# Moving the contiguous DRAM copies of streamed weights from the first step to steps 2 to 6

## The chip, the cores and the metric

The kernel runs on one core of a Trainium2 chip. The metric is the device time of one execution in microseconds; lower is better. Three runs of the kernel before took 3726.68, 3730.98 and 3731.62 us, median 3730.98.

## The reference, cut to what matters

Four layers run over a sequence of 2048 positions with 640 channels, alternating between a memory-augmented recurrent attention (A) and a local dilated attention (B):

```
x = x + A(layernorm(x)); x = x + B(layernorm(x))
x = x + A(layernorm(x)); x = x + B(layernorm(x))

A:  for each of 64 segments of 32 positions:
      h = concat(mem (8 rows), xs (32 rows))              # 40 x 640
      q, k, v = h @ Wq, h @ Wk, h @ Wv                    # 32 heads of 192
      o = softmax(mask(q k^T * 192**-0.5)) v ;  o = o @ Wo
      mem = o[:8] ; out = o[8:]
B:  32 heads of 20, each position looks at 8 positions, 2 apart
```

Both A layers use the same weights. The memory of a segment is made by the segment before it, so the segments come one after the other.

## The kernel before

One step of the outer loop in `run` takes one segment of the first A layer and, two steps behind it (`LAG = 2`), one segment of the second, side by side as two lanes of one tile (`ST`). There are 66 such steps with A work, numbered from 0 in the code, so the first step is step 0; one more step finishes layer B.

A's weights are 16 units each of Wq, Wk, Wv and Wo, cut into 64 "halves" of 128 x 1920 elements in bf16, 480 KB each. 31 of them (`RESIDENT`) stay in SBUF from step 0 on, in tiles `res`. The other 33 are streamed again in every step through `ring`, a pool of five buffers (`RING = 5`) with tiles named `wt`. `resident_halves` chooses the streamed ones so that they lie evenly along the step's work: it walks the list `PLAN` in the order in which PE uses the halves and drops one whenever enough columns of work have gone by.

A half in its original place in DRAM is strided: `load_direct` reads it as rows of 384 elements from Wq, Wk and Wv, five to a partition, or of 640 elements from Wo, three to a partition. In step 0 the kernel loads all 64 halves that way. Each streamed half is then written once from its ring buffer to a contiguous DRAM tile `Wr[h]`, by a DMA that GpSimd (POOL) issues (L238). From step 1 on, the streamed halves are read from `Wr[h]` (L240), one run of 3840 bytes per partition. All loads are issued by SyncE (SP), in one queue (L225, L240, and L251 for the input x).

A ring buffer may be loaded again only when PE has read its half and, where there is a copy out of it, when that copy has landed. The order of PE's work is written out by hand in `PLAN` (`manual_schedule` for PE); the order on the other engines comes from the scheduler of the tile framework. POOL has other work too, in the same in-order queue as its DMA issues: the squares for the layer norms (`sq`, L283, used by `ln1` and `ln2`), one lane of `prod` (L445) and copies into `ST`, `kh` and `vh`. Other lines that are spoken of below: L313 (q and k), L361 (v), L395 (the output projection, `acc`), L405 and L402 (the cast of the new memory from `acc` into `ST`, which ends a step), L485 (DVE reductions of layer B).

Of the kernel before, what the change touches and what calls it, by code (L numbers as in the profile page):

```python
# [41 lines left out]
BPAD = (BW - 1) * BDIL  # L42
SCB = float(BDH) ** -0.5
LAG = 2

N_HALVES = 64
N_RESIDENT = 31
# [24 lines left out]
def resident_halves():  # L72

    order, t = [], 0
    for what, i in PLAN:
        for h in ([2 * i, 2 * i + 1] if what == "q" else [{"v": 32, "o": 48}[what] + i] if what in "vo" else [None]):
            t += COLUMNS.get(what, 0)
            if h is not None:
                order.append((h, t))
    kept, n = set(), 0  # L80
    for h, at in order:
        if (N_HALVES - N_RESIDENT) * at >= (n + 0.5) * t:
            n += 1
        else:
            kept.add(h)
    assert len(kept) == N_RESIDENT
    return kept


RESIDENT = resident_halves()  # L90


def window(ap, l):
# [23 lines left out]
class Kernel:  # L117
# [109 lines left out]
    def half(self, h):  # L227
        if h in self.resident:
            return self.resident[h]
        if h in RESIDENT:  # L230
            t = self.res.tile([P, HALF], BF16, name=f"res{h}")
            self.load_direct(t, h)
            self.resident[h] = t
            return t
        t = self.ring.tile([P, HALF], BF16, name="wt")
        if self.step == 0:
            self.load_direct(t, h)
            self.nc.gpsimd.dma_start(out=self.Wr[h][:, :], in_=t[:, :])  # L238
        else:
            self.nc.sync.dma_start(out=t[:, :], in_=self.Wr[h][:, :])  # L240
        return t
# [156 lines left out]
    def finish_step(self):  # L398
        nc, s = self.nc, self.step
        nxt = self.ST[(s + 1) % 2]  # L400
        if s + 1 == LAG:
            nc.vector.tensor_copy(out=nxt[:, :, 0, 0:NM], in_=self.acc[:, :, 0, 0:NM])  # L402
# [7 lines left out]
        else:  # L410
            ra = self.zero[:, :, :]
        rb = self.x2[:, :, :] if s >= LAG else self.zero[:, :, :]
        for l, r in ((0, ra), (1, rb)):
# [34 lines left out]
    def b_logits(self):  # L448
# [8 lines left out]
        src = ps[:, :, :]  # L457
        for l, at in ((0, 1), (1, 1 + LAG)):
            if self.step == at:
# [27 lines left out]
    def b_wo(self):  # L487
# [6 lines left out]
        if s <= self.n_seg:  # L494
            x2 = self.w2.tile([P, NCH, SEG], BF16, name="x2")
            nc.vector.tensor_tensor(out=x2[:, :, :], in0=ps[:, :, 0, :], in1=self.xr[:, :, 0, :], op=ALU.add)  # L496
            self.x2_next = x2
        k = s - 1 - LAG
        if k >= 0:
# [12 lines left out]
    def store(self):  # L512
        nc = self.nc
        k = self.step - 1 - LAG
        if k < 0 or k % 4 != 3:
# [9 lines left out]
    def run(self):  # L525
        nc, tc = self.nc, self.tc
        self.resident, self.xt, self.vts, self.ots = {}, {}, {}, {}
        self.Wr = {h: self.dram.tile([P, HALF], BF16, name=f"Wr{h}") for h in range(N_HALVES) if h not in RESIDENT}
        self.kh = self.vh = None
        self.x2 = self.x2_next = None  # L530
        self.step = 0
        with tc.manual_schedule(engines={PE}):
# [3 lines left out]
            self.alpha_x(0)  # L536
            n_steps = self.n_seg + LAG
            attend = {"q": self.qk, "s": self.scores, "t": self.p_transpose, "v": self.v, "pv": self.pv, "o": self.o}
# [80 lines left out]
```

## Time and profile before

| what | value |
|---|---|
| median of three runs | 3730.98 us |
| span of the profiled execution | 3732.1 us |
| PE busy | 3430.9 us, 92% |
| DVE busy | 2077.9 us, 56% |
| DMA, SyncE's queue | 1091.82 MB, 86.2% of 16 engines' span |
| DMA, POOL's queue | 16.22 MB, 1.1% |
| mean DMA rate | 301 GB/s |
| mean granted TensorE clock | 0.984 |

The profiled execution is given by its span from the first to the last instruction; no other time of that execution is shown, and the span lies 0.5 us above the slowest of the three runs. A busy share is the share of the span in which an engine has at least one instruction under way. The DMA share is the mean busy share of the core's 16 DMA engines; it can read a little over 1. The granted clock is the share of TensorE's full clock. A time "to landing" runs from the issue of a DMA to the completion of its transfer. In a list of groups "x33" counts instructions, and in a list of waits the three numbers are the total wait in us, how many, and the longest.

### The profile page before, as it was taken

Reading aid. Unit: us, or ns where it says so; the run is one execution under the profiler, and the core shown is the slowest. Engines: PE = TensorE matmul, PEld = TensorE weight load, DVE = VectorE, ACT = ScalarE, POOL = GpSimd, SP = SyncE. Lnnn points to the kernel's source line nnn. Section 1 sums busy time; section 2 is a strip of 40 time slices with the busy share of each in tenths; the row PEclk is TensorE's granted clock in tenths of the full one; section 3 lists DMA queues with packets and bytes.
Section 4 is the critical chain, followed back from the end, with each engine's and each line's share of the span. In section 5 each row is a group of like instructions: output and inputs, shape, how many; then the busy total and the mean of one; then the engine's idle time right before and its main releaser. Section 6 shows DMA issues by size and latency. Waiting matters only on the chain.

```text
span 3732.1 us, 170184 instructions
## 1 busy us (share of the span) xinstructions
PE 3430.9 (92%) x78045; PEld 2929.7 (79%) x78045; DVE 2077.9 (56%) x4858; ACT 1493.5 (40%) x3213; POOL 365.5 (10%) x467
## 2 busy tenths in 40 slices
PE   5799999999999999999999999999999999999997
PEld 3588788788788878778887887887888788788886
DVE  1355555655555555655556565555555555555555
ACT  1243444444444344444434444444443444444443
POOL 2110010011011001011100100100110010011000
PEclk7899999999999999999999999999999999999998
DMA  9988888888888889889888888888888888888885
GB/s 351 343 297 296 295 302 304 297 305 293 304 301 302 304 296 306 297 299 307 300 307 301 303 301 291 307 291 303 305 301 302 303 307 297 306 296 300 304 304 193
DMA packets 356064, 1121.56 MB, mean 301 GB/s; under 512 B 36424, under 2 KB 78032, under 8 KB 355344
## 3 DMA queue, kind: packets, MB, share of 16 engines
q1 hardware_dynamic: 350400, 1091.82, 86.2%
q0 software_dynamic: 2640, 16.22, 1.1%
q8 instruction: 610, 9.99, 1.1%
q10 hardware_dynamic: 2304, 2.62, 0.2%
q14 instruction: 110, 0.90, 0.1%
HBM read 1091.68 MB, written 18.84 MB: 298 GB/s over the span
## 4 chain that ended last, share of the span: by engine, by line
PE 66%; DVE 21%; DMA 7%; ACT 2%; issue 2%; SPq 1%; POOLq 0%; DVEq 0%; POOL 0%; ACTq 0%
PE qk_ps L313 23%; PE v_ps L361 18%; PE acc L395 11%; DVE oT L485 5%; DVE prod L483 4%; PE qkv_ps L438 4%; PE s_ps L331 3%; PE s_ps L325 2%; DVE vt L367 2%; PE o_ps L378 2%; DMA x_sb<-in_A_x_dram 2%; DMA wt<-Wr 2%; PE y_ps L492 1%; DVE sb L335 1%; DVE mx L337 1%
## 5 line engine op out<-in xcount | busy, mean ns | idle before, releaser
L315 ACT CAST QK<-qk_ps 128x480 bf16<-128x480 f32 x1056 | 586.9, 556 | 1197.9 <-PE qk_ps L313 1190.2
L313 PE MATMUL qk_ps<-ST,res 128*128 128x80 bf16 x17820 | 800.2, 203 | 56.1 <-DVE ST L405 21.3
L361 PE MATMUL v_ps<-wt,ST 128*128 128x384 bf16 x3630 | 706.2, 328 | 134.8 <-DVE vt L367 124.3
L313 PEld LDWEIGHTS <-res 128*128 128x128 bf16 x17820 | 724.8, 100 | 97.9 <-issue 49.4
L361 PEld LDWEIGHTS <-ST 128*128 128x128 bf16 x5280 | 475.0, 99 | 410.5 <-issue 150.3
L313 PE MATMUL qk_ps<-ST,wt 128*128 128x80 bf16 x13860 | 646.8, 203 | 15.8 <-DMA wt<-in_A_Wq_dram 8.0
L313 PEld LDWEIGHTS <-wt 128*128 128x128 bf16 x13860 | 575.9, 100 | 68.7 <-DMA wt<-in_A_Wq_dram 9.0
L367 DVE CAST vt<-v_ps 128x384 bf16<-128x384 f32 x528 | 289.8, 549 | 542.8 <-PE v_ps L361 541.4
L395 PE MATMUL acc<-ot,wt 128*128 128x80 bf16 x7920 | 375.8, 203 | 17.8 <-DMA wt<-in_A_Wo_dram 6.7
L395 PE MATMUL acc<-ot,res 128*128 128x80 bf16 x7920 | 364.3, 203 | 11.2 <-issue 6.0
L395 PEld LDWEIGHTS <-res 128*128 128x128 bf16 x7920 | 328.4, 100 | 42.0 <-DMA res<-in_A_Wo_dram 7.1
L365 ACT CAST vt<-v_ps 128x384 bf16<-128x384 f32 x528 | 250.1, 474 | 266.4 <-PE v_ps L361 262.2
L395 PEld LDWEIGHTS <-wt 128*128 128x128 bf16 x7920 | 317.7, 100 | 30.8 <-issue 8.6
L381 ACT CAST ot<-o_ps 128x480 bf16<-128x480 f32 x528 | 275.0, 560 | 162.2 <-PE o_ps L378 162.1
L485 DVE TENSOR_REDUCE oT<-prod 128x64 bf16<-128x512 bf16 x330 | 335.1, 1016 | 2.2
L361 PE MATMUL v_ps<-res,ST 128*128 128x384 bf16 x1650 | 328.4, 330 | 6.2 <-DMA res<-in_A_Wv_dram 4.2
L445 POOL TENSOR_TENSOR prod<-qT,kh 128x1280 bf16<-128x1280 bf16 x66 | 204.4, 3097 | 684.1 <-ACT kh L440 684.1
L335 DVE TENSOR_TENSOR sb<-s_ps,maskA 128x320 f32<-128x320 f32 x264 | 129.3, 490 | 212.3 <-PE s_ps L331 212.3
L283 POOL TENSOR_TENSOR sq<-x 128x160 f32<-128x160 bf16 x64 | 28.9, 452 | 2095.3 <-DVE x L496 2095.3
L483 DVE TENSOR_TENSOR prod<-bc_ps,vh 128x512 bf16<-128x512 f32 x330 | 222.8, 675 | 9.9 <-PE bc_ps L480 1.6
L353 ACT COPY PT<-pt_ps 64x320 bf16<-64x320 bf16 x264 | 110.9, 420 | 242.0 <-DVE PT L352 239.1
L341 DVE TENSOR_REDUCE sm<-sb 128x8 f32<-128x320 f32 x264 | 127.7, 484 | 107.2 <-ACT sb L339 107.2
(113 smaller groups left out, 3320.1 us busy)
## 6 DMA issues: line engine op xcount, KB each, us to landing
wt<-Wr SPq DMA_DIRECT2D x2145, 480.0 KB, 5.2
Wr<-wt POOLq DMA_DIRECT2D x33, 480.0 KB, 6.7
wt<-in_A_Wv_dram SPq DMA_DIRECT2D x11, 480.0 KB, 10.3
res<-in_A_Wk_dram SPq DMA_DIRECT2D x9, 480.0 KB, 10.7
res<-in_A_Wq_dram SPq DMA_DIRECT2D x9, 480.0 KB, 10.4
wt<-in_A_Wo_dram SPq DMA_DIRECT2D x8, 480.0 KB, 9.1
res<-in_A_Wo_dram SPq DMA_DIRECT2D x8, 480.0 KB, 10.0
wt<-in_A_Wq_dram SPq DMA_DIRECT2D x7, 480.0 KB, 11.0
```

The source lines that it names most:

```text
L313: nc.tensor.matmul(ps[:, 3 * k + m, :, :], lhsT=w[:, c, m * P:(m + 1) * P], rhs=st[:, c, :, 0:LT], start=(c == 0), stop=(c == NCH - 1))
L315: nc.scalar.copy(out=self.QK[i % NQK][:, 0:12 * LT], in_=ps[:, :, :, :].rearrange("p m l t -> p (m l t)"))
L335: nc.vector.tensor_tensor(out=sb[:, :, :], in0=sv, in1=self.maskA[:, :].unsqueeze(1).to_broadcast([P, 8, LT]), op=ALU.add)
L361: nc.tensor.matmul(ps[:, :], lhsT=st[:, c, :, :].rearrange("p l t -> p (l t)"), rhs=w[:, c, :], start=(c == 0), stop=(c == NCH - 1))
L365: nc.scalar.copy(out=vt[:, :], in_=ps[:, :])
L367: nc.vector.tensor_copy(out=vt[:, :], in_=ps[:, :])
L381: nc.scalar.copy(out=ot[:, :, :, :], in_=ps[:, :, :, :, :].rearrange("p j n l t -> p (j n) l t"))
L395: nc.tensor.matmul(self.acc[:, dc, :, :], lhsT=w[:, m % 3, dc * P:(dc + 1) * P], rhs=ot[:, m, :, :], start=(j == 0 and m == 0 and dc == 0) ...
L438: nc.tensor.matmul(ps[:, d, :, :], lhsT=self.wqkv[:, c, kind * D + d * P:kind * D + (d + 1) * P], rhs=self.xnB[:, c, :].rearrange("p (l t) ...
L445: eng.tensor_tensor(out=self.prod[:, :, l, :, :], in0=qT[:, :, l, :].unsqueeze(2).to_broadcast([P, NCH, BW, SEG]), in1=window(kh, l), op=A ...
L483: nc.vector.tensor_tensor(out=pv, in0=ps[:, :, :, :], in1=window1(self.vh, c), op=ALU.mult)
L485: nc.vector.tensor_reduce(out=self.oT[:, c, :].rearrange("p (l t) -> p l t", l=2), in_=pv.rearrange("p l w t -> p l t w"), op=ALU.add, axi ...
```

## The change

In step 0 no copy to `Wr` is made any more. The streamed halves are dealt out in their order of use to steps 1 to 5 (the second to the sixth step): the first to step 1, the second to step 2, the sixth to step 1 again. Until its step, a half is loaded by the strided `load_direct` in each step; in its step it is loaded that way and copied out of the ring buffer to `Wr[h]`; afterwards it is read from `Wr[h]`. So steps 1 to 5 make 7, 7, 7, 6 and 6 copies, and 33, 26, 19, 12 and 6 of their 33 streamed loads are strided. Which halves are resident, the number of copies, and the order of all work on PE, DVE and ACT stay as they are; POOL's and SyncE's queues change.

```diff
+COPY_STEPS = 5
...
-    kept, n = set(), 0
+    kept, copied = set(), {}
     for h, at in order:
-        if (N_HALVES - N_RESIDENT) * at >= (n + 0.5) * t:
-            n += 1
+        if (N_HALVES - N_RESIDENT) * at >= (len(copied) + 0.5) * t:
+            copied[h] = 1 + len(copied) % COPY_STEPS
         else:
             kept.add(h)
     assert len(kept) == N_RESIDENT
-    return kept
-RESIDENT = resident_halves()
+    return kept, copied
+RESIDENT, COPIED = resident_halves()
...
         t = self.ring.tile([P, HALF], BF16, name="wt")
-        if self.step == 0:
+        if self.step <= COPIED[h]:
             self.load_direct(t, h)
-            self.nc.gpsimd.dma_start(out=self.Wr[h][:, :], in_=t[:, :])
+            if self.step == COPIED[h]:
+                self.nc.gpsimd.dma_start(out=self.Wr[h][:, :], in_=t[:, :])
         else:
             self.nc.sync.dma_start(out=t[:, :], in_=self.Wr[h][:, :])
         return t
```

## Prediction

> **What bounds the kernel now.** I read the page first, then the busy time by stretch (the first step, the five steps after it, the steady part), then the DMA view of the first 150 us and of the steady part, then the waits and the chain in order of time around the first step's end. Steps are counted from 0 as in the code; the copies move from step 0 to steps 1 to 5. From the page:
>
> ```profile
> span 3732.1 us, 170184 instructions
> ...
> PE 3430.9 (92%) x78045; PEld 2929.7 (79%) x78045; DVE 2077.9 (56%) x4858; ACT 1493.5 (40%) x3213; POOL 365.5 (10%) x467
> ...
> wt<-Wr SPq DMA_DIRECT2D x2145, 480.0 KB, 5.2
> Wr<-wt POOLq DMA_DIRECT2D x33, 480.0 KB, 6.7
> ```
>
> PE is the steady bound, with DMA close behind. By stretch (busy us of PE, PEld, DVE, ACT, POOL; granted clock; DMA share; GB/s):
>
> ```profile
> 20.00:130.00 110.00, 66.02 (x862) 46.60 (x859) 15.35 (x34) 17.59 (x35) 15.12 (x28) 0.67 1.07 366
> ...
> 258.00:315.00 57.00, 52.80 (x1188) 45.02 (x1185) 31.81 (x75) 22.38 (x48) 5.08 (x6) 0.97 0.86 293
> ...
> 500.00:3000.00 2500.00, 2347.37 (x54036) 2013.67 (x54030) 1439.36 (x3372) 1031.62 (x2223) 229.82 (x273) 1.00 0.89 301
> ```
>
> Step 0 is DMA-bound: share 1.07, 366 GB/s, PE busy 60% at a clock of 0.67. Later DMA has about 0.18 of share left under that 1.07. What the bytes cost: the queues in the first 150 us, then SyncE's in the steady part (packets, MB, share of 16 engines):
>
> ```profile
> q1 hardware_dynamic: 40080, 37.04, 76.4%
> q0 software_dynamic: 2640, 16.22, 26.8%
> ```
> ```profile
> q1 hardware_dynamic: 218842, 743.46, 87.5%
> ```
>
> A copy (q0) takes 0.268 x 150 / 33 = 1.22 us of all 16 engines. A contiguous load takes 0.875 x 2500 / 743.46 MB = 2.94 us per MB, 1.45 us per half of 0.492 MB. The strided loads are the rest of the first q1 row: 37.04 MB less 6.2 MB that is contiguous (wqkv, wo, six early Wr loads), so 114.6 - 18.2 = 96.4 us for 30.8 MB, 1.54 us per half.
>
> Boundaries by the cast of acc into ST (L405; L402 once): 144.89, 202.17, 258.33, 314.89, 368.52, 422.13. Steps 1 to 5 take 277 us; a quiet step 53.6 us, or 8.2 us for five of its 33 streamed halves (53.6 x 5 / 33). PE's waits between 500 and 3000 us hold almost nothing for a load; SyncE's own waits, over the whole span, are for PE to free a buffer:
>
> ```profile
> PE acc L395 <- DMA wt<-Wr: 2.2, 3, 1.1
> ```
> ```profile
> SPq L240 <- PE qk_ps L313: 871.8, 712, 4.0
> ...
> SPq L240 <- DMA Wr<-wt: 13.3, 4, 5.4
> ```
>
> The second of those SyncE rows is the important one. It is a load that waits for a copy out of its own ring buffer. One such case stands at the end of step 0: the copy issues, its landing ends a SyncE wait of 5.37 us, and the load follows:
>
> ```profile
> 142.83 0.54 POOL L238 DMA_DIRECT2D Wr<-wt  x1 [7.07 <-DMA wt<-in_A_Wo_dram]
> ```
> ```profile
> L240 SPq EVENT_SEMAPHORE  x1: 5367/5367/5367, 143.8 to 143.8; - x1
> L240 SPq DMA_DIRECT2D wt<-Wr x1: 319/319/319, 149.2 to 149.2; - x1
> ...
> DMA to landing us min/median/max: 4.2/4.2/4.2
> ```
>
> **Step 0 loses 33 copies.** It stays DMA-bound: 64 halves and 3.3 MB of wqkv and wo remain. The saving is 33 x 1.22 = 40 us of DMA time at a share of 1.07: 38 us. Bounds: 16.22 MB at 366 GB/s is 44; at the low clock PE needs 66 of 110 us, so PE may start to bind and leave 30. I take 38.
>
> **DMA work moved.** Steps 1 to 5 get 7, 7, 7, 6, 6 copies, and 33, 26, 19, 12, 6 of their loads become strided. Step 1 then holds 33 x 1.54 + 7 x 1.22 = 59.4 us of DMA work, 55.5 us at a share of 1.07, against the 57.3 us that it takes now; step 5 holds 6 x 1.54 + 27 x 1.45 + 6 x 1.22 = 55.7, or 52.1 against 53.6. So bandwidth alone costs nothing to 2 us in all. I take 0 for it.
>
> **The new wait.** This is the term that decides. Copied halves are every fifth streamed half, and the ring has five buffers: within a step all copies come out of one and the same buffer. So the load of half n+5 waits until half n has landed and its copy has landed too. On SyncE all later loads queue behind that wait, as does an x load; PE waits for the load. One turn of this buffer is load plus copy. Bounds: the shortest load row 3.2 and shortest copy 6.0 give 9.2; the medians 10.6 (strided, step 0) and 6.7 give 17.3, but up to eight loads queue in step 0, and a blocked ring lets few queue. I take the pair shown above, met after such a block: copy 6.3 (issue 142.83, landing releases the load at 149.17), load 4.2, strided excess 0.1, hand-over 0.1: 10.7 us. It stands against 8.2 us of work, so 2.5 us a turn is uncovered; the ring's lead is used up in the first turn. Turns inside a step: 6 + 6 + 6 + 5 + 5 = 28, so 70 us. Between steps the copied buffer changes, and I count nothing. At 9.2 the term is 28; at 12.3 (5.2 + 6.7 + 0.4) it is 115.
>
> The Trainium skill (SBUF — State Buffer, section "SBUF: two separate sides", the "DVE blocks DMA" trap) says that GpSimd can't write descriptors for its DMAs while DVE runs an op that holds their shared port pair; no copy here has yet met a busy DVE, so the trace can't settle it.
>
> **POOL's order.** In the built order a copy stands before ln2's sq (L283) in step 1, whose half is used just before ln2: sq then comes about 0.54 + 0.45 us after that landing, and ssq, ln_ps and ST wait for it; 2 us once. Elsewhere prod (3.1 us) delays a copy only where the copy's load lands before about 17 us into the step; the ring's wait makes it later than that: nothing, at most 3 us a step if the ring is ahead.
>
> **The clock.** In step 0, with PE gaps of 1 to 4 us, the granted clock was 0.67; in 258:315 one gap of 2.0 us (at 278.8) stands beside a mean of 0.97, that is 1.7 us lost. Gaps of 2.5 us in 28 turns will cost some of it. But PE's slower work first eats its own wait, as load and copy don't wait for PE. Lower bound 0; upper bound the 0.67 of step 0: a step of 51 us PE time becomes 51 / 0.67 + 4 = 80 us against 53.6 + 14 = 68 by the ring, so 60 in all. Nearest row is 258:315: I take 0.4 us a turn, 11 us. The Trainium skill (TensorE: Matmul & The Clock Gate, Part 1) names an idle window of about 3.4 us for the drop to half clock. By it alone gaps of 2.5 us cost nothing and the sum would be 3765; the 2.0 us gap beside a mean of 0.97 speaks for the dearer reading.
>
> **Sum.** -38 + 70 + 2 + 11 = +45 us. The profiled span, 3732.1 us, lies 1.1 above the median of the runs, 3730.98, and just above the highest, 3731.62, so no visible time lies around it; 3731 + 45 = 3776.
>
> **Rivals.**
> A, faster: the copies fit in the DMA slack. It decides if a turn stays under 8.2 us. For it: the DMA work above, and the lead that makes PE wait only 2.2 us for these loads at L395 in 2500 us. Against it: copy and load rows whose shortest sum is 9.2. Time: 3731 - 38 + 2 = 3695. Chance 0.17.
> B, about the same: turns at their cheap end, 9.2 to 9.5 us: 28 to 36, with no clock loss: 3723 to 3731. Chance 0.08.
> C, slower yet by the clock: PE stays at step 0's 0.67 and its own work binds: 3776 - 11 + 60 = 3825. Chance 0.10.
> D, slower yet by the copy's start: its descriptors wait for the DVE operation under way, up to the 1.0 us of the reductions of L485; DVE is busy 58% in these steps and 14% in step 0. 28 x 1.0: 3804. [...] For it only DVE's share; against it prod on POOL, which keeps 3.03 to 3.11 us in every step beside that DVE. Chance 0.08.
> That the change doesn't happen is excluded: in the built order POOL issues 7, 7, 7, 6, 6 copies in these steps, and every fifth SyncE load waits for one.
>
> **How the numbers follow.** The forecast, a ring turn of 10 to 12.3 us, has 0.57 and its own range is 3750 to 3825. A measurement of this kernel can't tell less than about 0.2%, 7.5 us. Faster is A, 0.17; same is B, 0.08; slower is the rest, 0.75. The range for 8 in 10 leaves out A's lower part and the tail of C with the costliest turns: 3708 to 3840.
>
> **What would show it.** Step 0 should end near 107 us, with a DMA share still at 1.07. Steps 1 to 5 should take 65 to 72 us each, with SyncE waits on Wr<-wt of several us, about 30 of them, and PE waits on wt in the chain; from step 6 on all is as before. Copies should take 6 to 6.7 us to landing, the loads behind them 4 to 5. If steps 1 to 5 stay near 55 us, the ring step is wrong; if copies take over 7, D; if the clock in these steps is under 0.8, C.

## The result and the profile after

The changed kernel took 3785.41 us (median of four runs, 3780.86 to 3791.68) against 3731.3 us for the kernel before (median of four, the three runs shown above and one of 3737.43): ratio 1.0145, 95% interval 1.013 to 1.0159. It is slower by 54 us. The profiled execution of the changed kernel took 3784.84 us, its span is 3783.1 us. Lines in its code are one or two numbers higher than before: the copy is L240, strided loads L226, loads from Wr L242, the end of a step L407.

PE is busy for 3448.3 us, 91% of that span. The copies' row of the page after (KB each, median us to landing):

```profile
Wr<-wt POOLq DMA_DIRECT2D x33, 480.0 KB, 6.5
```

By stretch after: the inside of step 0, steps 1 to 5, and the steady part (busy us of PE, PEld, DVE, ACT, POOL; granted clock; DMA share; GB/s):

```profile
20.00:100.00 80.00, 57.96 (x868) 41.68 (x865) 15.27 (x34) 17.89 (x36) 0.00 (x0) 0.79 1.10 333
...
109.00:478.00 369.00, 289.77 (x5905) 236.73 (x5906) 160.14 (x374) 112.78 (x244) 43.20 (x63) 0.92 0.80 267
500.00:3000.00 2500.00, 2351.16 (x54181) 2017.80 (x54178) 1445.76 (x3389) 1037.14 (x2234) 230.14 (x273) 1.00 0.89 302
```

Step 0 is still DMA-bound (share 1.10) and the steady part is as it was. The five steps between have changed their nature. PE isn't at its bound there, and neither is DMA: its share has fallen to 0.80, from 0.86 to 0.90 in the five steps of the kernel before, although these steps move more bytes than before. Something makes both wait. By the cast of acc into ST, steps end at 109.0, 185.0, 260.6, 334.4, 404.1 and 478.1 us:

| stretch | before, us | after, us | difference |
|---|---|---|---|
| step 0 | 144.9 | 109.0 | -35.9 |
| steps 1 to 5 | 277.2 | 369.2 | +92.0 |
| step 6 to the end of the span | 3310.0 | 3305.0 | -5.0 |

SyncE's waits after name the cause: 32 loads wait for a copy out of their own buffer, 30 of them strided loads with 7.2 us each (total us, times, longest):

```profile
SPq L226 <- DMA Wr<-wt: 216.4, 30, 10.2
...
SPq L242 <- DMA Wr<-wt: 15.7, 2, 7.9
```

PE's waits after, between 90 and 480 us, are now mainly for loads; before, in steps 1 to 5, loads took 1.3 us of PE's waiting:

```profile
PE v_ps L363 <- DMA wt<-in_A_Wv_dram: 31.1, 20, 5.0
PE acc L397 <- DMA wt<-in_A_Wo_dram: 15.7, 10, 4.3
PE qk_ps L315 <- DMA wt<-in_A_Wq_dram: 11.4, 6, 3.4
PE qk_ps L315 <- DMA wt<-in_A_Wk_dram: 8.0, 7, 2.4
```

The turn of the copied buffer can be read off two queues in step 1. POOL's copies (start, us, engine, line; in brackets the idle time before and what ended it):

```profile
131.33 0.58 POOL L240 DMA_DIRECT2D Wr<-wt  x1 [4.85 <-DMA wt<-in_A_Wk_dram]
143.33 0.54 POOL L240 DMA_DIRECT2D Wr<-wt  x1 [11.42 <-DMA wt<-in_A_Wv_dram]
154.86 0.54 POOL L240 DMA_DIRECT2D Wr<-wt  x1 [10.99 <-DMA wt<-in_A_Wk_dram]
```

and SyncE's loads in the same stretch:

```profile
130.27 0.44 SPq L226 DMA_DIRECT2D wt<-in_A_Wk_dram  x1
139.17 0.37 SPq L226 DMA_DIRECT2D wt<-in_A_Wv_dram  x1
139.63 0.48 SPq L226 DMA_DIRECT2D wt<-in_A_Wo_dram  x1
140.20 0.44 SPq L226 DMA_DIRECT2D wt<-in_A_Wv_dram  x1
140.73 0.48 SPq L226 DMA_DIRECT2D wt<-in_A_Wq_dram  x1
141.30 0.94 SPq L226 DMA_DIRECT2D wt<-in_A_Wv_dram  x1
150.52 0.37 SPq L226 DMA_DIRECT2D wt<-in_A_Wk_dram  x1
```

The copy issued at 131.33 lands 7.8 us later, at 139.1. At 139.17 SyncE issues the load that waited for it, and behind it, within 2.2 us, the four loads that had stood in line. Then SyncE is idle for 8 us. The first load of the burst lands 3.9 us after its issue and is copied from 143.33; the next burst starts at 150.52. One turn, 11 to 12 us, carries five halves, for which a quiet step needs 8.2 us.

### The profile page after: what moved, and what is told of

The parts are those of the page before. It is cut to its first block, busy times and chain, and to the rows that moved or that the text cites. A ratio compares the mean times of both kernels' runs of the same rounds, so it can differ in the third digit from the quotient of the medians.

```text
span 3783.1 us, 170182 instructions
## 1 busy us (share of the span) xinstructions
PE 3448.3 (91%) x78045; PEld 2937.0 (78%) x78045; DVE 2078.8 (55%) x4858; ACT 1495.3 (40%) x3213; POOL 365.9 (10%) x467
## 4 chain that ended last, share of the span: by engine, by line
PE 64%; DVE 20%; DMA 10%; issue 2%; ACT 2%; SPq 1%; POOLq 0%; POOL 0%; DVEq 0%; ACTq 0%
PE qk_ps L315 23%; PE v_ps L363 17%; PE acc L397 10%; DVE oT L487 5%; DVE prod L485 4%; PE qkv_ps L440 4%; PE s_ps L333 2%; PE s_ps L327 2%; DMA Wr<-wt 2%; DVE vt L369 2%; PE o_ps L380 2%; DMA x_sb<-in_A_x_dram 2%; DMA wt<-in_A_Wv_dram 2%; DVE sb L337 1%; DVE mx L339 1%
## 5 line engine op out<-in xcount | busy, mean ns | idle before, releaser
L485 DVE TENSOR_TENSOR prod<-bc_ps,vh 128x512 bf16<-128x512 f32 x330 | 222.6, 675 | 19.4 <-PE bc_ps L482 11.1
```

Source lines behind the costliest of these rows:

```text
L485: nc.vector.tensor_tensor(out=pv, in0=ps[:, :, :, :], in1=window1(self.vh, c), op=ALU.mult)
```

## Experiments

The theories: **ring** (a load waits for the copy out of its own buffer, and copies in one buffer chain), **work** (what costs is the DMA work of copies and strided loads), **POOL** (GpSimd's part: its in-order queue, or descriptors held up by DVE). All diffs are against the changed kernel unless another base is named; ratios are to the kernel before, with 95% intervals.

**Copy out of another tile**

```diff
-        if self.step <= COPIED[h]:
+        if True:
...
-                self.nc.gpsimd.dma_start(out=self.Wr[h][:, :], in_=t[:, :])
+                self.nc.gpsimd.dma_start(out=self.Wr[h][:, :].rearrange("p (a b) -> p a b", a=4),
+                                         in_=self.lastq[:, 0:480].unsqueeze(1).to_broadcast([P, 4, 480]))
```

(`lastq` is the QK tile that was cast last.)

> This kernel makes the same 33 copies in the same steps, but out of a QK tile instead of the ring buffer, and what they write is never read: all streamed loads stay strided in every step. So the DMA work of the copies is there and the ring buffer is free of them. Ring theory (a load waits for the copy out of its own buffer, 11.5 us a turn against 8.2): steps 1 to 5 fall from 369 us to 275 to 295, the step after them needs nothing, total 3695 to 3715 if strided loads cost nothing in later steps. Bandwidth theory (33 copies and about 100 more strided loads are too much DMA work): steps 1 to 5 stay near 369 and the total near 3785 or above. POOL theory (copies delay sq and prod behind them on POOL): part of it stays, 3750 or more.

Steps 1 to 5 took 297.4 us, just over the range of the ring theory. The total, 3764.58 us (1.0107, 1.0084 to 1.0129), is 50 us above its range and lies where I had put the POOL theory. But the excess is in the later steps, where no copies are made: steps 8 to 65 average 55.28 us against 54.61 before, which the next run explains. With the ring buffer out of it, 33 copies of the same size cost little in their steps: 72 of the 92 us are gone.

**No copies**

```diff
-            copied[h] = 1 + len(copied) % COPY_STEPS
+            copied[h] = 1000
```

> No copy is ever made and Wr isn't used: every streamed half is loaded strided in each of the 66 steps. Ring theory: the first step is as in the changed kernel (109 us), steps 1 to 5 take 275 to 285 us, and later steps 53.6 to 55 us as before if the 6% dearer strided load is hidden under PE: 3690 to 3705. If strided loads cost time once the copies are gone (their work is 33 x 1.54 = 51 us of a 53.6 us step), 0.5 to 2 us a step: 3730 to 3825.

3740.16 us (1.0051, 1.0033 to 1.0069); steps 1 to 5 took 281.3 us, so strided loads cost 4 of the 92 us. Later steps averaged 55.19 us against 54.61 before (steps 8 to 65), 0.58 us each: the second of my two cases, at its cheap end. The steady stretch shows why there is little room (same columns as above):

```profile
500.00:3000.00 2500.00, 2326.14 (x53563) 1996.88 (x53606) 1425.04 (x3339) 1024.17 (x2209) 229.38 (x272) 1.00 0.98 298
```

DMA share is 0.98 here against 0.89, for hardly fewer bytes. The contiguous copies are worth about 60 x 0.58 = 35 us in later steps and 4 us in steps 1 to 5, and cost 36 us in step 0: some 3 us gained by the two traces. The runs say more: without copies the kernel is 15 us slower at the median, 12 to 26 by the interval (the traced execution of the kernel before, with a span of 3732 us, was slower than the median of 3725 beside these runs). So the copies pay for themselves in the kernel before, with little to spare.

**Seven copies in a row**

```diff
-            copied[h] = 1 + len(copied) % COPY_STEPS
+            copied[h] = 1 + len(copied) // 7
```

> Each step's copies are seven halves that follow one another instead of every fifth one (7, 7, 7, 7, 5), so all five buffers are copied once and two of them twice, and a step has two copied turns in a row instead of six. Ring theory: about 2 x 3.3 us, less a lead of 2 to 3 us, plus some queueing of five copies together: 4 to 10 us a step instead of 18, total 3715 to 3745. Bandwidth theory and POOL theory: the same copies per step, no change from 3785.

3727.13 us (1.0007, 0.9995 to 1.0019). Steps 1 to 5 took 65.5, 67.5, 64.2, 59.3 and 57.0 us, 36 us over before, where the changed kernel is 92 over. The number of copies and strided loads a step is nearly the same; only which halves are copied differs. SyncE's waits for copies:

```profile
SPq L226 <- DMA Wr<-wt: 75.4, 28, 8.8
```

As many waits as in the changed kernel, but 2.7 us each instead of 7.2: copies of neighbouring halves share one turn. The work theory has no room for this. The copies stand at other places in POOL's queue too, so for POOL's part the run with ScalarE below is the better one.

**Every fourth half**

```diff
-COPY_STEPS = 5
+COPY_STEPS = 4
```

> The copies go to four steps instead of five, so every fourth streamed half is copied and the copied buffer changes from copy to copy. Ring theory: a buffer that was copied is next loaded with a half that is not copied; the waits still join through SyncE's order (half n holds n+5, behind which n+8 lands, is copied and holds n+13): 7.1 + 4 + 3 x 1.6 + 0.3 = 16.2 us for eight halves that take 13.1, 12 to 13 us a step, 50 us in four steps: 3740 to 3755. Bandwidth theory: the same DMA work in four steps instead of five, 3785 or above.

3762.67 us (1.0104, 1.0081 to 1.0126). Steps 1 to 4 took 75.0, 74.4, 73.4 and 73.1 us, 18 us over before where I expected 12 to 13. So it is better than the changed kernel only because there are four such steps. POOL's queue shows the turn:

```profile
136.88 0.58 POOL L240 DMA_DIRECT2D Wr<-wt  x1 [4.38 <-DMA wt<-in_A_Wk_dram]
147.15 0.54 POOL L240 DMA_DIRECT2D Wr<-wt  x1 [9.69 <-DMA wt<-in_A_Wo_dram]
154.66 0.54 POOL L240 DMA_DIRECT2D Wr<-wt  x1 [6.98 <-DMA wt<-in_A_Wk_dram]
```

Two copies, eight halves, in 154.66 - 136.88 = 17.8 us, where 13.1 would do and I had 16.2. The waits join through SyncE's order although no buffer is copied twice in a row, as expected; the size was too small.

**One copy a step**

```diff
-COPY_STEPS = 5
+COPY_STEPS = 33
```

> One copy a step in 33 steps. Ring theory: no copied turn follows another in a step, so each copy delays one load by about 3 us, of which the ring's lead of 2 to 3 us takes most: 0.3 to 1 us a copy, 10 to 33 us; 33 steps have on average half of their loads strided, at 0.57 us a step for all of them (the run without copies): 9 us; step 0 saves 36: 3714 to 3737, near 3720. Work theory (a copy costs its 1.22 us of DMA wherever it lies, and 1.1 us when DMA is saturated): 33 to 40 plus 9 less 36: 3737 to 3745.

3762.94 us (1.0101, 1.0085 to 1.0117): outside both ranges. Steps 1 to 33 took 1876.6 us against 1809.5, so 2.0 us a copy; about 0.3 of it may be strided loads (half of 0.58). SyncE's loads still wait for copies, 4.7 us each:

```profile
SPq L226 <- DMA Wr<-wt: 131.5, 28, 8.5
```

I had thought that the ring's lead takes most of a lone late load. If a lone turn is as long as in the changed kernel, 11.6 us, it leaves 3.4 us uncovered, and the lead covered only about 1.7; neither the lead nor a lone turn was measured by itself. What the run does show: a copy alone in its step costs 2.0 us, against 2.8 in the changed kernel's chains (92 / 33), strided loads included in both, so chaining through one buffer is the smaller part of a copy's price.

**Five in a row, and all in one step**

```diff
-            copied[h] = 1 + len(copied) % COPY_STEPS
+            copied[h] = 1 + len(copied) // 5
```
```diff
-COPY_STEPS = 5
+COPY_STEPS = 1
```

> Five copies of five successive halves a step, in seven steps: each buffer is copied out once a step and no buffer twice in a row. Ring theory: one late turn a step, 3 to 6 us with five copies queueing: 21 to 42 us in seven steps, 2 us for strided loads, less 36: 3718 to 3739. If only the number of copies counted (92 us for 33 copies, as in the changed kernel): 3785.

> All 33 copies in the second step. Ring theory: every turn is a copied one, and each holds five loads and five copies, 13.8 us of DMA work or 12.9 at a share of 1.07: 13 to 15 us a turn, 86 to 99 us for the step instead of 57; less 36: 3724 to 3738. So the cost is paid once instead of five times although the number of copies is the same. If copies cost by their number (2.8 us each): 3785.

Five in a row: 3730.49 us (1.0006, 0.9994 to 1.0019). All in step 1: 3727.01 us (0.9999, 0.999 to 1.0008), that step 88.2 us instead of 57.3. Its stretch:

```profile
108.00:197.00 89.00, 62.76 (x1194) 50.47 (x1191) 33.52 (x81) 22.60 (x50) 22.70 (x39) 0.88 1.03 362
```

Here DMA is saturated as in step 0 of the kernel before (1.03, 362 GB/s). So 33 copies cost 31 us in one step, 36 in step 0, and 92 spread over five steps in one buffer each. What is paid for is late turns of the ring, not copies; copies that share a turn cost about 0.9 to 1.1 us each (31 / 33 to 36 / 33), near the 1.1 us of DMA time worked out for step 0.

**Copies issued by ScalarE**

```diff
-                self.nc.gpsimd.dma_start(out=self.Wr[h][:, :], in_=t[:, :])
+                self.nc.scalar.dma_start(out=self.Wr[h][:, :], in_=t[:, :])
```

> The changed kernel with the copies issued by ScalarE instead of GpSimd: nothing else differs. Theory that GpSimd's descriptors are held up by DVE: copies land in 5 us or less instead of 6.5, 1.5 us off each of 28 turns: 3743 or less. Ring theory with the copy's time set by the loads that stream beside it: copies still take 5.5 to 6.5 us, 3757 to 3785; ScalarE now waits for each load's landing before it goes on with its casts, which may cost as much again.

3757.62 us (1.0088, 1.0075 to 1.0101), steps 1 to 5 352.0 us. The copies' landing times with ScalarE, min, median and max:

```profile
DMA to landing us min/median/max: 4.7/6.3/8.7
```

At the median that is 0.2 us less than with GpSimd, not 1.5. The turn fell from 11.6 to 10.9 us, mostly between a load's landing and the copy's issue: 0.03 us on ScalarE, 0.48 on GpSimd (means of the turns whose landings the two traces have, 19 and 24). Steps 1 to 5 became 17 us shorter, as the ring theory has it for a shorter turn; GpSimd's descriptors account for no more than the 0.2 us.

**Copies from DRAM to DRAM**

```diff
-                self.nc.gpsimd.dma_start(out=self.Wr[h][:, :], in_=t[:, :])
+                src, k = self.source(h)
+                self.nc.sync.dma_start(out=self.Wr[h][:, :].rearrange("p (a b) -> p a b", a=k), in_=src)
...
-        with tc.manual_schedule(engines={PE}):
+        with tc.manual_schedule(engines={PE, mybir.EngineType.SP}):
```

> The changed kernel, but each copy goes from the weight in DRAM to Wr in DRAM, right behind that half's load in SyncE's queue (which here runs in program order), and no ring buffer is held. Ring theory: no load waits for a copy out of its buffer; left is what uncoupled copies cost beside the loads, 16 us in five steps by the run that copied from QK, and a few us for strided loads; step 0 saves 36: 3705 to 3720. If the cost of a copy is its DMA work whatever waits for it (1.1 us each, 36 us): 3726 to 3735. If ring waits were not the cause: 3785.

3699.32 us (0.9924, 0.9907 to 0.994): faster than both kernels, by 27 us against the kernel before, and by some 2.2% or 82 us against the changed kernel if the two ratios are set side by side. Its steps 8 to 65 average 54.58 us, as before (54.61). Steps 1 to 5:

```profile
109.00:399.00 290.00, 261.71 (x5900) 223.21 (x5906) 158.85 (x373) 112.98 (x244) 25.36 (x30) 0.99 1.02 342
```

290 us, 13 more than before, with DMA at a share of 1.02 and 342 GB/s and PE's clock at 0.99. Beside the changed kernel's 369 us at a share of 0.80 this is the clearest pair: more DMA traffic (each copy also reads DRAM again), and 79 us less. No ring buffer is held. The copies also moved to another queue, and SyncE's runs in program order; each by itself, another queue was worth 17 us in these steps (ScalarE, above) and program order nothing (the control below, on the kernel before).

**Wo never copied, and both together**

```diff
--- kernel before
-        if self.step == 0:
+        if self.step == 0 or h >= 48:
             self.load_direct(t, h)
-            self.nc.gpsimd.dma_start(out=self.Wr[h][:, :], in_=t[:, :])
+            if h < 48:
+                self.nc.gpsimd.dma_start(out=self.Wr[h][:, :], in_=t[:, :])
```

> The kernel before, with the 8 streamed Wo halves loaded strided in every step and never copied, so step 0 makes 25 copies. Work theory: 8 x 1.1 = 9 us less in step 0; the Wo rows of 1280 bytes cost no more DMA time than contiguous ones, so later steps lose 0 to 0.1 us each: 3717 to 3726. If strided loads of any kind cost what the run without copies showed (0.57 us a step for 33, so 0.14 for 8): 9 us lost again, 3726.

> Both: copies from DRAM to DRAM in steps 1 to 5, and none of Wo. If the two gains add: 25 copies at 0.5 us instead of 33, 3700 to 3716. If later steps pay for Wo: as the run with DRAM to DRAM copies alone.

On the kernel before: 3721.77 us (0.9986, 0.9974 to 0.9998), step 0 ends at 139.0 instead of 144.9 us. On the changed kernel with copies from DRAM to DRAM, and again none of Wo: 3701.62 us (0.9929, 0.9911 to 0.9947), no better than with all 33 of them. The first gains 5 us at the median (0.7 to 10 by the interval), as expected. In the second, where no buffer waits for the copies, eight fewer bring nothing that can be measured.

**Control: SyncE in program order**

```diff
--- kernel before
-        with tc.manual_schedule(engines={PE}):
+        with tc.manual_schedule(engines={PE, mybir.EngineType.SP}):
```

> Control: the kernel before with SyncE's queue in program order, nothing else. All theories: the loads already stand nearly in that order, 3720 to 3732, no difference that can be measured; if it differs, the runs with copies behind the loads have to be read against this one.

3727.77 us (1.0001, 0.9987 to 1.0014): no difference. The changed kernel itself was not run with SyncE in program order.

## Why the prediction was right, point by point

The forecast was 3776 us; the time measured is 3785. The mechanism stands: loads wait for the copy out of their own buffer, and a turn of that buffer is longer than the work that covers it. That the sum came within 9 us owes something to luck. Steps 1 to 5 were forecast to lose 83 us (70 + 2 + 11) and lost 92: the turns, 25 us too cheap, were made up for in part by 11 us for the clock that found no place of their own, and what comes after these steps took 5 us less, which nothing here explains.

- **Step 0.** -38 forecast, -35.9 found; it ends at 109.0 us, not 107. The share went up to 1.10 while the rate went down to 333 GB/s: loads without copies move fewer bytes per busy time here than the mix with copies.
- **The turn of the ring** is the term that was mis-sized. Over the 24 turns whose copies lie 9.5 to 14 us apart and whose landings the trace has, it is 11.63 us, not 10.7 (all 28 turns inside steps average 11.57): copy 6.43 (6.3 forecast), SyncE's issue 0.06, load 4.66 (4.3), and 0.48 until POOL issues the next copy (0.1 for both hand-overs). The load of the first burst rows, at 3.9 us, was below my value; in other turns the load took up to 8.9 us. 28 turns of 3.4 us uncovered give 95, against 70 forecast. That is close to the 92 us that steps 1 to 5 took longer, which leaves nothing for the clock.
- **The clock.** 11 us forecast; it was granted at 0.92 in these steps, and PE is busy for 290 us where five windows of before sum to 258. But the four parts of a turn hold no PE work, so the slower PE fills time in which it would have waited. My term had no place of its own, as far as the sum of turns shows; no run held the clock up while leaving the turns. The Trainium skill (TensorE: Matmul & The Clock Gate, Part 1) puts the drop to half clock after an idle window of about 3.4 us. Read as a rule on single gaps, that does not agree with this trace. Between 109 and 478 us it has 15 stretches at half clock, and 11 of them follow PE gaps none of which is over 3.0 us: 0.51 is granted from 310.4 to 313.8 us behind a gap of 2.38 us, and 0.50 from 395.7 to 399.1 us behind one of 2.84. A gap of 3.39 us, up to 192.6 us, is followed by full clock. So the prediction's dearer reading, by the 2.0 us gap of before, was right about the clock, though not about its price.
- **DMA work**, taken as 0, costs 13 to 16 us where nothing waits for the copies (13 in the run from DRAM, strided loads included; 16 in the run from QK, against the run without copies). Neither run shows how much of it the changed kernel pays outside the turns; the sum of turns leaves no room for it.
- **POOL's order.** 2 us forecast; PE waits 1.1 us for ssq in ln2 and ln1 together in these steps.
- **Rival A**, copies hidden in the slack, is refused for this kernel, but it is true of the copies themselves: taken off the ring buffer they are all but hidden. The point that decides was right, a turn against 8.2 us.
- **Rival B** needs turns of 9.2 to 9.5 us; the mean turn is 11.63. **Rival C** would show a clock under 0.8; the lowest step has 0.88. **Rival D** would show copies over 7 us; the median is 6.5 beside a DVE busy 43% of the time, against 6.7 before in step 0, and ScalarE's copies, which the trace has on a hardware queue (q10) instead of GpSimd's software queue (q0), take 6.3. Copies of before had met DVE operations too, 25 of the 33 by their times, but at a DVE share of 14%. The trap that the Trainium skill (SBUF — State Buffer, section "SBUF: two separate sides") describes for DVE operations in a two-port mode isn't seen here: with DVE at 43%, GpSimd's copies take 0.2 us longer than ScalarE's. Whether any DVE operation of these steps ran in such a mode no run shows, nor that the reduction of L485, from which D took its 1.0 us, ever holds up a descriptor.

The forecast of 65 to 72 us for each of these steps was low for four of five (69.7 to 76.1); six turns of 0.9 us more come to 5.6 us, which is about what was missing.

## What to carry to other kernels

Where a ring buffer must be written out before it can be loaded again, its turn is load plus write-out plus the hand-overs, whatever bandwidth is free; compare that turn with the work that the other buffers cover, and look whether successive write-outs fall on the same buffer. Spreading such write-outs evenly can be the worst choice: each then pays for a late turn of its own (2.0 us a copy here), and a period equal to the ring's length chains all of them besides (2.8), while a bunch shares its turns and costs little more than its DMA time (0.9 to 1.1). The best of the ways tried holds no buffer at all, here a second read from DRAM (0.4).

## What the runs showed of the hardware that was not expected

- In the turns of the changed kernel, SyncE's load follows the landing of the copy that it waited for after 0.05 us in most cases, but GpSimd's copy follows the landing of its load after 0.28 to 0.54 us (ScalarE's: 0.03).
- TensorE's granted clock fell to half behind PE gaps of 1.4 to 3.0 us at the longest in 11 of its 15 stretches at half clock in steps 1 to 5.
- In step 0, DMA moved 366 GB/s at a share of 1.07 with loads and copies mixed, and 333 GB/s at 1.10 with strided loads alone; so the mean share says little of the rate that is left.
- DMA at a share of 1.02 for 290 us, with 342 GB/s, cost PE 13 us in five steps, as long as no load had to wait for a buffer.
